# Moving the output stores of a fused attention and FFN kernel to ScalarE, with four loads in flight, DMA transposes in one more step and no decay columns in the last

## The chip, the cores and the metric

The kernel runs on one core of a Trainium2 chip. The metric is the device time of one execution in microseconds (us), as the median of several runs. The profiler's span, from the first to the last record, is shorter than the device time (span 201.4, time 203.12 in the profiled run of the kernel before). Engines: TensorE (PE in the profile; PEld is its weight load), VectorE (DVE), ScalarE (ACT), GpSimd (POOL), SyncE (SP). A q behind the name (SPq, ACTq) is the engine's instruction queue when it issues a DMA.

## The reference

A gated linear attention runs over 768 positions in 4 batches and 8 heads of 48 channels. Its output, 3072 tokens of 384 values, goes through a gated FFN of hidden width 1536.

```python
f = 1.0 / (1.0 + np.exp(-f_logit))
for t in range(S):                                   # S = 768, B = 4, H = 8, D = 48
    state = f[:, :, t, :, None] * state + np.einsum('bhd,bhe->bhde', k[:, :, t], v[:, :, t])
    y[:, :, t] = np.einsum('bhd,bhde->bhe', q[:, :, t], state)
x = y.transpose(0, 2, 1, 3).reshape(B * S, H * D)    # 3072 x 384
out = (np.maximum(x @ w_gate, 0.0) * (x @ w_val)) @ w_out
```

## The kernel before

The kernel takes the 768 positions in six steps of 128 (called step 0 to 5, `c` in the code). In each step and batch it makes prefix sums of the log gates, scaled q and k ("hats"), transposes of these, scores, the output x and a new state; then the FFN of that step for all four batches. Attention of later steps and FFN of earlier ones are interleaved on TensorE.

The kernel first lists its operations with estimated durations, and a list scheduler in the kernel (called the builder here) places them. It works out a plan with a start and an end for every operation, and from that plan fixes one instruction order per engine. On the chip the waits between the lists are semaphores. In the trace of the kernel before, what waited held up what was behind it in its list: ScalarE stood 3.69 us before an exponential whose gate load had not landed (it started at 127.27 us), and the next relu of its list started at 128.39.

Loads of q, k, v and the gate logits f cover two batches each (128 x 16 x 48 floats). A load is paced by the third load before it: the builder does not place it before the planned landing of that one. This "pace" is used in the plan only. There is no semaphore for it.

```python
def load(n, c, b0, b1, after=(), paced=(), eng="SP"):
    ...
    op = add(eng, lambda: e.dma_start(dst, src), [], [f"{n}{c % NL}_{b}" for b in range(b0, b1)],
             occ=..., lat=..., prio=..., after=after, follows=[last] if last else [], paced=paced)
    dma(op, f"{n}{c % NL}_{b0}{b1}", flow, (6.0 if (c, n, b0) == (1, "v", 0) else 2.0) if c else 0.8)

loads.append(load(n, c, b, b + load_batches, loads[-flight:][:1]))      # flight = 3
```

x goes to the FFN transposed. Up to step 3 TensorE transposes it and VectorE copies it out; from step 4 on, a DMA transpose issued by SyncE does it:

```python
if c < first_xbar_x:                                  # first_xbar_x = 4
    ...
    te.transpose(x16()[:, kt * C:(kt + 1) * C], xn[ni][:, kt * C:(kt + 1) * C], ident[:])   # 3 of them
    ...
else:
    op = add("SP", lambda: sy.dma_start(xT[xi][:, :, b * C:(b + 1) * C], xn[ni][:, :], transpose=True), ...)
```

Prefix sum and decay columns, and the store of an output block behind ScalarE's copy of it:

```python
te.matmul(bc.ap[:, 0:HD], tri[:, :], bn[:, :, 0:D])
for p in range(NP):                                   # NP = 4, the decay columns
    mm = te.matmul(bc.ap[:, HD + p:HD + p + 1], bn[:, 2*p:2*p + 2, :]..., ones[:, :])
...
add("ACT", lambda ...: sc.activation(osb[oi][:, n0:n1], o.ap[:, 0:n1 - n0], AF.Copy), ...)
op = add("SP", lambda ...: sy.dma_start(dst, osb[oi][:, n0:n1]), ..., occ=0.2, lat=0.9, prio=P)
```

## Time and profile before

| | before |
|---|---|
| time, median of the first 3 runs | 203.14 us (202.06 to 204.03) |
| span of the profiled run | 201.4 us |
| TensorE busy | 191.7 us, 95% |
| other engines busy | DVE 54%, ACT 57%, POOL 38% |
| bytes read and written in HBM | 25.95 and 4.72 MB |

The page cuts the span into 40 slices and gives the busy share of each in tenths. TensorE is at 9 nearly everywhere after 40 us, so what counts is where it is not. Its waits from 40 us on are few, and the longest is 2.2 us. The profiled run (203.12 us, mean clock 0.992) counts as slow, being 1.5% above the fastest run of this kernel in any set (200.11). Its mean clock of 0.992 is one stretch of 3.41 us at half clock (131.14 to 134.56 us), 1.7 us lost; 17 of the 32 runs of this kernel in the rounds of the experiments had a mean clock of 0.992 or less. In the wait views below the columns are: who waited for whom, the sum in us, how often, and the longest. The profile's own lines of this kernel stand in the prediction.

### The profile page before, as it was taken

How to read it: one execution, taken by the hardware profiler on the slowest of the kernel's cores; microseconds unless marked ns; L12 is line 12 of the kernel's file. 1: busy time of each engine (PE TensorE's matmuls, PEld its weight loads, DVE VectorE, ACT ScalarE, POOL GpSimd, SP SyncE). 2: the span in 40 equal slices, each digit the busy share in tenths (PEclk: the TensorE clock that was granted, in tenths of full speed). 3: DMA queues.
4: the chain of work that ended last, by engine and by line, in shares of the span. 5: the costliest groups of instructions: out<-in, count | busy, mean ns of one | idle time of the engine just before them, and what ended most of it. 6: DMA issues, size and time to landing. Idle time of an engine off the chain costs nothing.

```text
span 201.4 us, 4570 instructions
## 1 busy us (share of the span) xinstructions
PE 191.7 (95%) x1813; PEld 124.4 (62%) x1813; DVE 107.9 (54%) x212; ACT 115.2 (57%) x264; POOL 77.3 (38%) x111
## 2 busy tenths in 40 slices
PE   7989899799999999999999999599999999999995
PEld 5766688676789787855664655245555555444564
DVE  7268575565098988628586846135462334433210
ACT  2976868716678686877677572744354333443412
POOL 5189203563559687772858364053000000000000
PEclk9999999999999999999999999969999999999999
DMA  4999999999999999999989998979222001111113
GB/s 119 234 223 196 198 200 180 204 231 210 230 232 232 158 247 189 221 198 230 192 161 234 159 199 186 189 156 221 77 63 59 24 19 39 39 39 42 39 39 117
DMA packets 116660, 31.35 MB, mean 156 GB/s; under 512 B 109600, under 2 KB 116640, under 8 KB 116640
## 3 DMA queue, kind: packets, MB, share of 16 engines
q1 hardware_dynamic: 112656, 27.53, 67.2%
q0 software_dynamic: 3984, 3.54, 11.0%
q8 instruction: 14, 0.23, 0.5%
q14 instruction: 6, 0.05, 0.1%
HBM read 25.95 MB, written 4.72 MB: 152 GB/s over the span
## 4 chain that ended last, share of the span: by engine, by line
PE 73%; DMA 13%; SPq 8%; ACT 2%; POOL 2%; issue 1%; DVE 0%
PE ps L766 37%; PE ps L789 22%; SPq L399 7%; DMA q_in<-in_q_dram 4%; DMA wv<-in_moe_w_val_dram 4%; PE ps L638 3%; DMA f_in<-in_f_logit_dram 3%; DMA v_in<-in_v_dram 3%; PE ps L615 2%; PE ps L677 2%; PE ps L582 2%; PE ps L673 2%; PE ps L718 1%; PE ps L699 1%; PE ps L584 1%
## 5 line engine op out<-in xcount | busy, mean ns | idle before, releaser
L777 DVE TENSOR_TENSOR gT<-relu,ps 128x256 bf16<-128x256 bf16 (+1 forms) x96 | 52.2, 552 | 59.9 <-PE ps L766 37.2
L766 PE MATMUL ps<-xT,wg 128*128 128x256 bf16 (+1 forms) x288 | 63.1, 328 | 0.3 <-DMA wg<-in_moe_w_gate_dram 0.3
L773 ACT ACTIVATE relu<-ps 128x256 bf16<-128x256 f32 (+1 forms) x96 | 46.3, 490 | 29.1 <-PE ps L766 28.7
L766 PE MATMUL ps<-xT,wv 128*128 128x256 bf16 (+1 forms) x288 | 62.6, 326 | 0.0
L789 PE MATMUL ps<-wo,gT 128*128 128x384 bf16 (+2 forms) x300 | 52.5, 320 | 0.0
L789 PEld LDWEIGHTS ps<-wo,gT 128*128 128x128 bf16 x300 | 27.7, 98 | 17.4
L766 PEld LDWEIGHTS ps<-xT,wg 128*128 128x128 bf16 x288 | 27.0, 98 | 15.6 <-DMA wg<-in_moe_w_gate_dram 0.6
L644 DVE TENSOR_TENSOR ptm<-ps,tri 128x512 bf16<-128x512 f32 x48 | 30.6, 684 | 10.8 <-PE ps L638 10.7
L766 PEld LDWEIGHTS ps<-xT,wv 128*128 128x128 bf16 x288 | 26.1, 98 | 16.0 <-ACT relu L773 0.2
L809 ACT ACTIVATE osb<-ps 128x384 f32<-128x384 f32 (+2 forms) x25 | 11.8, 477 | 30.6 <-PE ps L789 30.5
L602 POOL TENSOR_TENSOR hats<-k_in,expo 128x384 bf16<-128x384 f32 x20 | 20.0, 1000 | 20.3 <-ACT expo L591 20.3
L605 POOL TENSOR_TENSOR hats<-q_in,expo 128x384 bf16<-128x384 f32 x20 | 20.0, 1002 | 2.2 <-DMA q_in<-in_q_dram 2.2
L734 POOL TENSOR_TENSOR st<-ssum,dec 128x384 bf16<-128x384 f32 x16 | 13.3, 830 | 16.2 <-DVE ssum L732 16.2
L455 PE MATMUL ps<-zeros 128*128 128x256 bf16 x89 | 13.0, 301 | 1.1 <-DVE zeros L359 1.1
L691 ACT ACTIVATE xn<-ps 128x384 bf16<-128x384 f32 x20 | 9.8, 488 | 7.1 <-PE ps L677 7.1
L558 POOL CAST vpad<-v_in 128x384 bf16<-128x384 f32 x24 | 12.0, 515 | 3.0 <-DMA v_in<-in_v_dram 2.8
L572 ACT ACTIVATE f_in<-f_in 128x768 f32<-128x768 f32 x10 | 8.4, 838 | 6.4 <-DMA f_in<-in_f_logit_dram 6.4
L591 ACT ACTIVATE expo<-ps 128x384 f32<-128x384 f32 x20 | 9.8, 492 | 3.0 <-PE ps L584 2.9
L455 PEld LDWEIGHTS ps<-zeros 128*128 128x128 bf16 x89 | 9.0, 107 | 3.0 <-DVE zeros L359 1.1
L638 PE MATMUL ps<-qkT 48*128 48x128 bf16 x192 | 8.9, 226 | 1.2 <-ACT qkT L528 0.8
L593 ACT ACTIVATE expo<-ps 128x384 f32<-128x384 f32 x20 | 10.0, 498 | 0.0
L732 DVE TENSOR_TENSOR ssum<-ps,st 128x384 f32<-128x384 f32 x16 | 8.8, 551 | 1.1 <-PE ps L718 0.9
(71 smaller groups left out, 158.3 us busy)
## 6 DMA issues: line engine op xcount, KB each, us to landing
out_dram<-osb SPq DMA_DIRECT2D x23, 192.0 KB, 2.2
f_in<-in_f_logit_dram SPq DMA_DIRECT2D x10, 384.0 KB, 6.2
k_in<-in_k_dram SPq DMA_DIRECT2D x10, 384.0 KB, 6.4
q_in<-in_q_dram SPq DMA_DIRECT2D x10, 384.0 KB, 4.5
v_in<-in_v_dram SPq DMA_DIRECT2D x10, 384.0 KB, 4.8
wg<-in_moe_w_gate_dram POOLq DMA_DIRECT2D x3, 384.0 KB, 7.1
wv<-in_moe_w_val_dram POOLq DMA_DIRECT2D x3, 384.0 KB, 7.4
wo<-in_moe_w_out_dram POOLq DMA_DIRECT2D x3, 384.0 KB, 7.2
```

Of the source, the lines that this page charges most:

```text
L399: op = add(eng, lambda: e.dma_start(dst, src), [], [f"{n}{c % NL}_{b}" for b in range(b0, b1)], occ=(0.8 if eng == "SP" else 0.3) * (b1 - ...
L455: op = add("PE", lambda: te.matmul(cold.ap[:, 0:256], zeros[:, 0:128], zeros[:, :]), ["zeros"], [cold], occ=0.22 if i < 17 else 0.11, lat= ...
L558: add("POOL", lambda: gp.tensor_copy(vout, vin[:, b, :, :].rearrange("p (n j) d -> p n j d", j=2)), [f"v{li}_{b}", f"vpad{vi}"], [f"v_{vi} ...
L602: add("POOL", lambda: gp.tensor_tensor(hk, kin[:, b, :, :], ex[:, 1, :].rearrange("p (h d) -> p h d", h=H), ALU.mult), [f"k{li}_{b}", f"ex ...
L605: add("POOL", lambda: gp.tensor_tensor(hq, qin[:, b, :, :], ex[:, 0, :].rearrange("p (h d) -> p h d", h=H), ALU.mult), [f"q{li}_{b}", f"ex ...
L638: mm = te.matmul(s.ap[:, p * C:(p + 1) * C], qkT[qi][lo:lo + D, 1, p, :], qkT[qi][lo:lo + D, 0, p, :])
L644: add("DVE", lambda j=j, s=s: ve.tensor_tensor(ptm[mi][:, j, :, :], s.ap[:, :].rearrange("p (n t) -> p n t", n=NP), mask, ALU.mult), [s, " ...
L734: add("POOL", lambda: gp.tensor_tensor(t4(s_new), t4(tmp), rate, ALU.mult), [key] + dk, [f"S{b}_{c % 2}"], prio=P + 8, **pool_t(HD))
L766: mm = te.matmul(bank.ap[:, 0:n], wt[:, kt, j * 128:(j + 1) * 128], xT[xi][:, kt, n0:n1], start=(kt == 0), stop=(kt == NK - 1))
L773: add("ACT", lambda: sc.activation(relu[ri][:, 0:n], gate.ap[:, 0:n], AF.Relu), [gate], [f"relu{ri}"], prio=P, **act_t(n))
L777: add("DVE", lambda: ve.tensor_tensor(gT[gi][:, j, n0:n1], relu[ri][:, 0:n], val.ap[:, 0:n], ALU.mult), [val, f"relu{ri}"], [f"gT{gi}_{j}_ ...
L789: mm = te.matmul(o.ap[:, 0:n1 - n0], gT[gi][:, j, b * C:(b + 1) * C], wo[:, j, n0:n1], start=(j == 0), stop=(j == NJ - 1))
```

## The change

Four things were changed together. The stores are issued by ScalarE right behind its own copy, so that SyncE no longer stands waiting for that copy (15 waits in the kernel before, 47.9 us in all, the longest 5.5). Four loads are in flight instead of three. x of step 3 goes by DMA transposes too. The last step, which makes no new state, leaves out its decay columns.

```diff
-    flight = 3
+    flight = 4
-    first_xbar_x = 4
+    first_xbar_x = 3
+    STORE = 'ACT'
...
-                te.matmul(bc.ap[:, 0:HD], tri[:, :], bn[:, :, 0:D])
-                for p in range(NP):
+                mm = te.matmul(bc.ap[:, 0:HD], tri[:, :], bn[:, :, 0:D])
+                for p in range(NP if c < NC - 1 else 0):
...
-            chain("cum", ..., occ=0.29, lat=PE_L,
+            chain("cum", ..., occ=0.29 - (0.12 if c == NC - 1 else 0), lat=PE_L,
...
-            op = add("SP", lambda ...: sy.dma_start(dst, osb[oi][:, n0:n1]), ...,
-                     occ=0.2, lat=0.9, prio=P)
+            op = add(STORE, lambda ...: (sy if STORE == "SP" else sc).dma_start(dst, osb[oi][:, n0:n1]), ...,
+                     follows=first_stores if g == 0 else [], occ=0.2 if STORE == "SP" else 0.4,
+                     lat=0.9 if STORE == "SP" else 1.2, prio=P)
...
+    first_stores = [tails["loadSP"]] if '0' == "1" else []      # empty
```

More of the change, by code (lines that the diff above doesn't have):

```diff
@@ L586, in cum @@
                 return mm
-            chain("cum", "PE", cum, ["tri", "ones", f"bneg{bi}", f"bn{bi}_{bj}"], [bc], occ=0.29, lat=PE_L,
+            chain("cum", "PE", cum, ["tri", "ones", f"bneg{bi}", f"bn{bi}_{bj}"], [bc], occ=0.29 - (0.12 if c == NC - 1 else 0), lat=PE_L,
                 prio=P, opens=[bc])
@@ L811, in ffn_out @@
             dst = bass.AP(tensor=out.tensor, offset=(b * S + g * C) * DM + n0, ap=[[DM, C], [1, n1 - n0]])
-            op = add("SP", lambda dst=dst, oi=oi, n0=n0, n1=n1: sy.dma_start(dst, osb[oi][:, n0:n1]), [f"osb{oi}_{x}" for x in TAIL[:-1] if n0 <= x < n1], [f"out{g}_{b}_{n0}"],
-                     occ=0.2, lat=0.9, prio=P)
+            op = add(STORE, lambda dst=dst, oi=oi, n0=n0, n1=n1: (sy if STORE == "SP" else sc).dma_start(dst, osb[oi][:, n0:n1]), [f"osb{oi}_{x}" for x in TAIL[:-1] if n0 <= x < n1], [f"out{g}_{b}_{n0}"],
+                     follows=first_stores if g == 0 else [], occ=0.2 if STORE == "SP" else 0.4, lat=0.9 if STORE == "SP" else 1.2, prio=P)
             dma(op, f"osb{oi}_{n0}", 0.45 * (n1 - n0) / DM)
+    first_stores = [tails["loadSP"]] if '0' == "1" else []
     OJ = 4
@@ L864, in bass_hgrn2_outer__then__ffn_reglu_kernel @@
             op.val = n
-    stores = [op for op in order["SP"] if op.writes and op.writes[0].startswith("out")]
+    stores = [op for op in order[STORE] if op.writes and isinstance(op.writes[0], str) and op.writes[0].startswith("out")]
     def run(name, eng):
```

## The prediction

> **What bounds the kernel now.** I read the page first (engines, slices, chain), then the stretches in time, then the chain and the SyncE queue around the one place where TensorE stands still.
>
> ```profile
> PE 191.7 (95%) x1813; PEld 124.4 (62%) x1813; DVE 107.9 (54%) x212; ACT 115.2 (57%) x264; POOL 77.3 (38%) x111
> PE   7989899799999999999999999599999999999995
> PEclk9999999999999999999999999969999999999999
> DMA  4999999999999999999989998979222001111113
> ```
>
> TensorE is busy 95% of the span. There is one dip inside, in slice 26 (126 to 131 us), followed by the only slice with a lower granted clock. The DMA row is at 9 until about 137 us. The kernel therefore has three stages: a start to 40 us, which hangs on loads and weights; a middle to about 137 us, in which attention and FFN are interleaved while the loads stream in; and a pure FFN tail, where TensorE is at 10.00 of 10 us in each stretch. The change leaves the start alone: the first output store is at 48.3 us and the first paced load is one of step 2. The stretches of the middle:
>
> ```profile
> 110.00:115.00 5.00, 5.00 (x57) 2.98 (x56) 4.23 (x7) 2.30 (x4) 1.93 (x4) 1.00 0.88 162
> ...
> 120.00:125.00 5.00, 4.73 (x48) 2.79 (x49) 3.30 (x6) 1.09 (x2) 3.10 (x5) 1.00 0.93 204
> 125.00:130.00 5.00, 2.81 (x28) 1.42 (x26) 0.69 (x1) 2.73 (x6) 0.00 (x0) 1.00 1.00 169
> 130.00:135.00 5.00, 5.00 (x40) 2.52 (x39) 1.25 (x2) 3.21 (x8) 2.08 (x3) 0.66 0.94 194
> ```
>
> The columns are window, length, busy time of PE, PEld, DVE, ACT and POOL with counts, clock, DMA share and GB/s. TensorE loses 2.19 us between 125 and 130 and then runs at 0.66. The chain of waits says why:
>
> ```profile
> 118.80 0.61 ACT relu L773
> 119.42 1.22 SPq L812
> 120.64 0.04 issue
> 120.68 1.19 SPq L707
> 121.87 0.04 issue
> 121.92 5.33 DMA f_in<-in_f_logit_dram
> 127.25 0.02 issue
> 127.27 0.84 ACT f_in L572
> ```
>
> The gate load for the second half of step 5 is issued at 121.92. In SyncE's in-order queue it stands behind an output store (which waited for ScalarE, then took 1.22 us) and behind a DMA transpose of 1.19 us. It lands 5.33 us later. ScalarE, also in order, sits 3.69 us on that load with a relu behind it. TensorE comes to the prefix sum of this batch and waits 2.19 us for it, although some 70 us of FFN work stand behind. This is a blocked order, not a lack of work.
>
> [...]the later loads have rows of 48 floats (192 B), and 109600 of the 116660 packets are under 512 B, with at most 247 GB/s in a slice.[...] clock 0.68 from 129.7 to 135[...]
>
> **The change, part by part.**
>
> *No decay columns in step 5.* Four matmuls of one column for each of 4 batches go. The chain shows such a four at 0.09 us (117.93), so 4 x 0.09 = 0.36 us of TensorE. They precede the tail, and TensorE is packed there: all of it counts.
>
> *x of step 3 by DMA transposes.* Four times three TensorE transposes go, 0.19 us a three in the chain (95.96): 0.76 us on a packed engine, so it counts. VectorE loses 4 copies of 0.354 us, which lie beside. Added are 4 DMA transposes on SyncE: the existing eight take 1.18 to 2.09 us of its queue and land after a median of 2.4 us (up to 5.2). That is 5 to 8 us more in SyncE's queue between 88 and 110 us.
>
> *Stores move to ScalarE.* From SyncE go the stores that lie before the late load: 1.15, 0.58, 1.24 and 1.84 us between 78 and 122 us, 4.8 us together. Over that stretch (78.9 to 121.9) the queue's entries sum to 40.9 of 43.0 us, waits included: SyncE is as full as the DMA engines. The four new transposes take back what the four stores give, so SyncE's total hardly falls; what goes is SyncE waiting on copies in ScalarE. ScalarE gains 25 issues. In the quiet tail one takes 0.34 us on SyncE; with the wait for its own copy I estimate 0.5 to 1.2 us of ScalarE each, some 10 us for the dozen in the middle. ScalarE has 7.2 to 7.9 of 10 us busy between 60 and 110, so it becomes some 0.85 full; that should cost TensorE 0 to 1.5 us through late relus and exponentials, say 0.7. In the tail ScalarE is 40% busy and nothing is lost. At the very end the store of the 256 columns is issued by ScalarE between the last two copies: the first ends at 198.78, the matmuls at 199.04, so an issue of 0.34 us from about 198.85 could delay the last copy by 0.1 to 0.2 us[...].
>
> *Four loads in flight.* The pacing is no semaphore; it only sets where the builder places a load in SyncE's order. One more in flight puts the late load about one slot earlier, and the loads of step 5 go out 2 to 6 us apart (107.1, 109.2, 115.1, 118.2, 121.9). It would pass a transpose that waited on GpSimd (the entry of 4.31 us at 110.73) rather than sit behind it. DMA ran at only 162 GB/s in that stretch, so there is room. Three us earlier would cover the idle 2.19 us and with it the throttled stretch: 5.3 us at 0.68 loses 5.3 x 0.32 = 1.7 us. Worth 3.9 us if the gap goes.
>
> Sum: 0.36 + 0.76 = 1.1 us almost certain; 3.9 us for the gap, which I give six chances in ten, or about 2.5 when partial success is counted; minus 0.7 for ScalarE. That is 1.1 + 2.5 - 0.7 = 2.9, and 203.14 - 2.9 = 200.2. I move it to 200.0, because the parts look tuned together. The measured 203.14 against the span of 201.4 is a fixed difference that I carry over.
>
> **Rivals.**
> 1. *The gap stays, because the DMA engines are the bound.* For: their row is at 9 to 137 us, and four transposes are added. Against: 162 to 169 GB/s in the two stretches before and in the gap, against 230 elsewhere. Time: 203.14 - 1.1 + 0.7 = about 202.7; if the gap grows by 2 us, 204 to 205.
> 2. *ScalarE becomes the new blocker.* Its store waits for its own copy, then issues[...], and the relus behind it starve TensorE of its four FFN banks. For: issues of 1.2 us are seen on SyncE. Against: a store is 128 rows of 1536 B on a ring of its own, and TensorE hardly waits for a relu now (under 0.3 us in all). With 12 stores at 0.2 us of TensorE it eats 2.4 us: 201 with the gap closed, 204 with it open.
> 3. *All goes well:* the gap closes and ScalarE costs nothing: 203.14 - 5.0 = 198.1.
> 4. *The new order moves the blockage.* The builder places everything anew, so another load, or an x transpose of step 3, may block. Time as in rival 1.
>
> **Range and chances.** Rival 3 is nearly the floor, as nothing else inside is idle; I put the low end at 197.9. The high end, 203.0, is the gap kept and the small parts won. Faster by over 2% means below 199.08: the gap closed and at most 1 us given back, about one in three. Slower than 207.2 needs a new blockage of over 4 us: 0.06.
>
> **What would show it.** Right: slice 26 at 9 and the clock row without the 6; the gate load of step 5's second half landing 3 us or more before its prefix sum; 64 single-column matmuls in place of 80, 24 TensorE x transposes for 36, 12 x transposes by DMA for 8; stores on ScalarE's queue at 0.35 to 1.2 us each; TensorE busy down by 2 to 3 us (work, and throttled time). Wrong: TensorE idle again for over 1 us anywhere between 45 and 150; waits of TensorE on relu or exponentials summing to more than 1.5 us; or a start that differs from 40.5 us.

## More of the kernel before

The plan's times are estimates of the kernel's author, not measurements.

```python
    # Plan.schedule: when an operation has been placed, its users become ready
    for u in op.users:
        u.n_left -= 1
        if u.deps[op] == "order":
            at = op.start
        elif u.eng == op.eng == "PE":
            at = op.start + op.occ
        else:
            at = op.end                      # for a load: its planned landing
            ...
        u.ready = max(u.ready, at)
```

## The result, and the profile after

The changed kernel took 210.36 us in the median of 6 runs (208.02 to 212.47), the kernel before 203.58 us in the same rounds. The ratio is 1.0305 with a 95% interval of 1.0228 to 1.0382: 3% slower. Here and below, a ratio is the mean time of one kernel's fast runs over that of the other's fast runs of the same rounds, so it is not quite the ratio of the medians quoted.

The page of the changed kernel, its engine line and three of its slice rows:

```profile
PE 194.6 (94%) x1785; PEld 124.6 (60%) x1785; DVE 107.6 (52%) x208; ACT 116.1 (56%) x264; POOL 77.1 (37%) x111
PE   7999899799999995999995979999999999999995
PEclk9999999999999999799999799999999999999999
DMA  4999999999999898999979889999131111111113
```

The one dip of before after 40 us (slice 26) has become three (slices 16, 22 and 24, counted from 1 as in the prediction), and the clock falls twice. TensorE is busy 2.9 us longer with 28 instructions fewer. The stretches show where the time lies. First the kernel before, then the changed kernel; the first number pair is the window and its length, then busy time and instruction counts of PE, PEld, DVE, ACT and POOL, the clock, the DMA share and GB/s:

```profile
40.00:150.00 110.00, 106.90 (x1128) 69.88 (x1129) 68.18 (x128) 68.94 (x168) 59.74 (x75) 0.98 0.98 193
150.00:201.40 51.40, 49.03 (x272) 25.97 (x270) 15.13 (x22) 18.46 (x34) 0.00 (x0) 1.00 0.14 47
```

```profile
40.00:150.00 110.00, 103.37 (x1057) 66.36 (x1058) 65.47 (x121) 67.22 (x163) 59.23 (x75) 0.97 0.99 192
150.00:207.00 57.00, 54.50 (x319) 29.02 (x316) 17.43 (x26) 21.18 (x39) 0.00 (x0) 1.00 0.15 49
```

At 150 us the changed kernel still has 54.50 us of TensorE work ahead, the other 49.03. These 5.5 us are the whole difference of the spans (207.0 - 201.4 = 5.6). So the loss arises in the middle, between 40 and 150 us; start and tail run as before. The DMA engines moved the same 192 to 193 GB/s there, so no bandwidth was gained or lost.

Who held TensorE up? The first fence below is ScalarE's wait on gate loads in the kernel before from 40 us on; the second has the same line and TensorE's three longest waits in the changed kernel:

```profile
ACT f_in L572 <- DMA f_in<-in_f_logit_dram: 6.4, 3, 3.7
```

```profile
ACT f_in L573 <- DMA f_in<-in_f_logit_dram: 12.4, 6, 5.5
...
PE ps L639 <- issue: 3.3, 2, 2.3
...
PE ps L767 <- ACT relu L774: 2.1, 1, 2.1
...
PE ps L616 <- POOL hats L606: 1.2, 1, 1.2
```

ScalarE waits twice as long and twice as often for the gate loads. The chain of waits of the changed kernel shows how such a wait gets to TensorE (start, duration, what):

```profile
72.51 7.25 DMA f_in<-in_f_logit_dram
79.75 0.02 issue
79.78 0.84 ACT f_in L573
80.62 0.02 issue
80.64 0.39 ACT relu L774
81.04 0.05 issue
81.08 0.83 PE ps L767 x6
```

A gate load of step 3 lands at 79.75. ScalarE's list has the exponential of that gate first and a relu of the FFN behind it. TensorE's next matmuls, of L767, wait for this relu, and TensorE has been idle for 2.1 us when they start at 81.08. The relu had nothing to do with the load: it only stood behind it.

The longest gap is another one, before the scores:

```profile
112.03 0.62 PE L639 MATMUL ps<-qkT 48*128 48x128 bf16 x16 [2.26 <-issue]
```

"issue" means that the profile names no releaser. The scores read DMA transposes of scaled q and k; the last one before the gap was issued at 107.76, and those of this stretch land 3.3 to 4.2 us from issue, which fits 112.03. The chain of waits leads from that transpose back over GpSimd and ScalarE to a gate load that landed at 101.87. So this gap, too, goes back to a late gate load, by a longer way; that is inferred from the chain. The gap of 1.06 us at 122.33 stands before scores as well; it was not followed up.

The stores themselves do what was intended. Here is ScalarE's timeline of the changed kernel around one of them:

```profile
107.86 0.49 ACT L810 ACTIVATE osb<-ps 128x384 f32<-128x384 f32 x1
108.38 0.36 ACTq L813 DMA_DIRECT2D out_dram<-osb  x1
108.79 0.60 ACT L774 ACTIVATE relu<-ps 128x512 bf16<-128x512 f32 x1 [0.44 <-PE ps L767]
```

Copy, issue, next relu: from the end of the copy (108.35) to the relu 0.44 us pass, 0.36 of them for the issue.

The decisive reading is a comparison that the page does not make: the builder's plan against the chip. ScalarE starts the exponential of each gate load when that load is there (landed at 127.25 us, started at 127.27, for the last one of the kernel before) or a little later. The planned starts are those that the builder works out when it makes the order; the seen starts are in ScalarE's timeline (us; two loads per step):

| gate load of | 2 | 3 first | 3 second | 4 first | 4 second | 5 first | 5 second |
|---|---|---|---|---|---|---|---|
| before, planned | 63.4 | 72.1 | 82.6 | 92.5 | 101.9 | 112.4 | 123.3 |
| before, seen | 65.0 | 72.3 | 83.1 | 93.0 | 102.6 | 113.3 | 127.3 |
| changed, planned | 61.7 | 69.4 | 76.6 | 85.3 | 96.1 | 106.7 | 117.6 |
| changed, seen | 62.5 | 70.8 | 79.8 | 89.6 | 101.9 | 115.9 | 129.2 |

(The first column is the second load of step 2.) Before, plan and chip agree within 1.6 us up to the last load, which is 4 us late: that is the one gap of before. With the change the plan counts on loads up to 7 us earlier than before. On the chip they come at most 3.3 us earlier in steps 2 to 4 and 2 to 3 us later in step 5. By the end, the plan is 11.6 us ahead of the chip, and every engine's order was made for that plan.

The builder also gives each kernel's planned span. Run again on the kernels' code, it says 198.0 us for the kernel before, 197.4 for the changed one, 198.1 for the kernel before with the fourth load alone and 200.6 for it with the x transposes alone. It thus saw a cost of the x transposes (2.6 us) and none of the fourth load.

### The profile page after: what moved, and what is told of

It reads as the page before. It is cut to its first block, busy times and chain, and to the rows that moved or that the text cites. A ratio compares the mean times of both kernels' runs of the same rounds, so it can differ in the third digit from the quotient of the medians.

```text
span 207.0 us, 4512 instructions
## 1 busy us (share of the span) xinstructions
PE 194.6 (94%) x1785; PEld 124.6 (60%) x1785; DVE 107.6 (52%) x208; ACT 116.1 (56%) x264; POOL 77.1 (37%) x111
## 3 DMA queue, kind: packets, MB, share of 16 engines
q10 hardware_dynamic: 3600, 4.72, 7.2%
HBM read 25.95 MB, written 4.72 MB: 148 GB/s over the span
## 4 chain that ended last, share of the span: by engine, by line
PE 41%; DMA 25%; SPq 24%; ACT 5%; POOL 2%; issue 2%; ACTq 0%
PE ps L767 23%; SPq L400 21%; PE ps L790 15%; DMA f_in<-in_f_logit_dram 11%; DMA q_in<-in_q_dram 4%; DMA wv<-in_moe_w_val_dram 4%; DMA wo<-in_moe_w_out_dram 3%; DMA v_in<-in_v_dram 3%; SPq L625 2%; ACT f_in L573 2%; ACT relu L774 1%; POOL hats L606 1%; PE ps L639 1%; ACT bneg L576 1%; PE ps L583 1%
## 5 line engine op out<-in xcount | busy, mean ns | idle before, releaser
L767 PE MATMUL ps<-xT,wg 128*128 128x256 bf16 (+1 forms) x288 | 63.2, 328 | 2.4 <-ACT relu L774 2.1
L767 PE MATMUL ps<-xT,wv 128*128 128x256 bf16 (+1 forms) x288 | 63.5, 329 | 0.0
L790 PE MATMUL ps<-wo,gT 128*128 128x384 bf16 (+2 forms) x300 | 53.7, 325 | 0.0
L790 PEld LDWEIGHTS ps<-wo,gT 128*128 128x128 bf16 x300 | 28.4, 99 | 18.2 <-issue 1.0
L767 PEld LDWEIGHTS ps<-xT,wg 128*128 128x128 bf16 x288 | 26.9, 98 | 19.4 <-ACT relu L774 2.2
L767 PEld LDWEIGHTS ps<-xT,wv 128*128 128x128 bf16 x288 | 26.8, 98 | 17.3 <-issue 0.3
L456 PE MATMUL ps<-zeros 128*128 128x256 bf16 x89 | 14.1, 318 | 1.1 <-DVE zeros L360 1.1
L592 ACT ACTIVATE expo<-ps 128x384 f32<-128x384 f32 x20 | 9.8, 490 | 5.5 <-PE ps L585 5.3
L456 PEld LDWEIGHTS ps<-zeros 128*128 128x128 bf16 x89 | 9.5, 113 | 3.6 <-DVE zeros L360 1.1
L639 PEld LDWEIGHTS ps<-qkT 48*128 48x128 bf16 x192 | 5.5, 94 | 8.1 <-issue 6.5
```

Source lines behind the costliest of these rows:

```text
L456: op = add("PE", lambda: te.matmul(cold.ap[:, 0:256], zeros[:, 0:128], zeros[:, :]), ["zeros"], [cold], occ=0.22 if i < 17 else 0.11, lat= ...
L639: mm = te.matmul(s.ap[:, p * C:(p + 1) * C], qkT[qi][lo:lo + D, 1, p, :], qkT[qi][lo:lo + D, 0, p, :])
L767: mm = te.matmul(bank.ap[:, 0:n], wt[:, kt, j * 128:(j + 1) * 128], xT[xi][:, kt, n0:n1], start=(kt == 0), stop=(kt == NK - 1))
L790: mm = te.matmul(o.ap[:, 0:n1 - n0], gT[gi][:, j, b * C:(b + 1) * C], wo[:, j, n0:n1], start=(j == 0), stop=(j == NJ - 1))
```

## The experiments

Theory A was that the fourth load in flight moves the plan, not the loads, and that the order built on it blocks TensorE. Theory B was that the four added x transposes do it through SyncE's queue. Theory C was that the stores on ScalarE do it.

### One part at a time

**flight4_alone.** The kernel before with

```diff
-    flight = 3
+    flight = 4
```

> The kernel before with four loads in flight, nothing else of the change. Theory A (with four in flight the builder's own plan expects the gate load of step 5's second half at 114.6 us instead of 123.3, the real loads come no earlier, so every engine's order is built for loads that are not there and TensorE blocks): 207 to 211 us, 2 to 4% slower, TensorE idle 4 us or more between 45 and 150. Theory B (the four added x transposes on SyncE do the damage): 201 to 204, about the same as before. Theory C (stores on ScalarE do it): about the same as before.

Measured: 210.84 us against 203.02, ratio 1.0367 (1.0303 to 1.0432). This one number does more damage than the whole change. ScalarE's wait on the gate loads, and in the next fence the stretch of the middle:

```profile
ACT f_in L572 <- DMA f_in<-in_f_logit_dram: 16.1, 7, 3.6
```

```profile
40.00:150.00 110.00, 100.23 (x1076) 64.92 (x1074) 64.50 (x124) 65.88 (x162) 57.68 (x73) 0.98 0.95 188
```

TensorE does 6.7 us less in the middle than before (100.23 against 106.90), in many small waits. Theory A had said that the loads come no earlier, and in this it was wrong: the late gate load of step 5 did come earlier, as the prediction had it: its exponential started at 122.97 instead of 127.27. But the plan had moved it by more, from 123.3 to 114.6. Earlier loads were no gain, since the order had been drawn up for still earlier ones.

**xdma_alone.** The kernel before with

```diff
-    first_xbar_x = 4
+    first_xbar_x = 3
```

> The kernel before with the x transposes of step 3 by DMA, nothing else. Theory A: 202 to 205 us, within 1.5% of before, since the plan keeps the pacing (load planned at 127.5). Theory B: 207 to 211, since SyncE's queue gets 5 to 8 us longer and the loads stand behind transposes that wait for ScalarE. Theory C: about the same as before.

Measured: 207.17 us against 203.02, ratio 1.0207 (1.0136 to 1.0279). Theory A alone does not cover this: there is a second cost. The chain of waits of this run shows it:

```profile
115.31 0.22 ACT xn L691
115.53 3.66 DMA xT<-xn
119.19 0.05 issue
119.24 1.46 PE ps L766 x3
```

The x of step 3 is ready at 115.53, its DMA transpose lands 3.66 us later, and what TensorE's list has next is matmuls that read it: it stands idle 3.96 us, then takes 1.46 us for three matmuls that otherwise take 0.65, as the clock is at half from 115.3 to 122.1 (a mean of 0.86 from 100 to 125 us). (This profile is of the slowest of the four runs. It also has a gap of 2.34 us at 44 us, on a v load, before any transpose of x of step 3; that one can hardly be the change's.) With TensorE's own transposes the same step took 0.19 us and a VectorE copy of 0.35 us.

**stores_act_and_decay.** The changed kernel with

```diff
-    flight = 4
+    flight = 3
-    first_xbar_x = 3
+    first_xbar_x = 4
```

> The changed kernel with three loads in flight and x of step 3 by TensorE: only the stores on ScalarE and the missing decay columns remain. Theories A and B: 201 to 203.5 us, 0 to 1% faster than before (0.36 us of matmuls saved, SyncE freed of stores). Theory C: 206 or more, with TensorE waiting for relus behind store issues.

Measured: 202.45 us against 203.02, ratio 0.9966 (0.9913 to 1.0020): the same. Theory C falls.

**after_flight3.** The changed kernel with

```diff
-    flight = 4
+    flight = 3
```

> The changed kernel with three loads in flight again. Theory A: most of the loss comes back, 202 to 205 us. Theory B: it stays at 207 to 211. Theory C: it stays at 207 to 211.

Measured: 206.40 us against 203.02, ratio 1.0160 (1.0079 to 1.0242). About half of the loss comes back; that is less than theory A had expected (202 to 205). What stays fits the x cost: TensorE waits 2.4 us for x in this profile.

**after_xpe.** The changed kernel with

```diff
-    first_xbar_x = 3
+    first_xbar_x = 4
```

> The changed kernel with x of step 3 by TensorE again: four in flight, stores on ScalarE, no decay columns. Theory A with the x transposes as a second cost that overlaps the first: 207.5 to 210.5 (flight4_alone less 0.4 to 1). If the two costs simply add: 206 or less.

Measured: 208.30 us against 202.53, ratio 1.0271 (1.0182 to 1.0361). Next to four in flight, the x transposes cost no more than the noise (1.0305 with them, in another set of rounds). The two costs overlap: the changed kernel's profile has no wait of TensorE for x over 0.2 us.

### Is it the order, or are four loads in flight bad in themselves?

The next two kernels change only what the builder believes. A load's users are counted ready some time after (or before) its planned landing; the pacing of the loads themselves keeps the planned landing.

```diff
-                    at = op.end
+                    at = op.end + (op.slack if u.deps[op] != "pace" else 0.0)
...
         tails["load" + eng] = op
+        op.slack = (0, 0, 1, 2, 3, 4)[c]       # flight4_honest, beside flight = 4
+        op.slack = (0, 0, -2, -3, -3, -3)[c]   # flight3_hopeful, beside flight = 3
```

**flight4_honest**

> flight4_alone (210.8 us) with the same four loads in flight and the same transfers, but the builder is told that a load of step 2, 3, 4, 5 is usable 1, 2, 3, 4 us after its planned landing; its plan then starts the gate exponentials within 2 us of where the chip started them in flight4_alone (planned 81.1, 91.0, 102.0, 112.8, 124.7; seen 80.0, 90.1, 101.8, 113.2, 123.0). Theory A (the order, built on loads planned too early, is what blocks TensorE): 201 to 204.5 us. Rival D (four loads in flight[...] hold up transposes and stores, whatever the order): 208 or more.

Measured: 203.78 us against 202.53, ratio 0.9992 (0.9857 to 1.0126). The ratio rests on two fast runs, 200.77 and 203.74; the other two, 203.82 and 204.52, count as slow. Most of the 3.7% is gone; up to 1.3% may be left. The middle of the profiled run, the fastest of the four:

```profile
40.00:150.00 110.00, 106.94 (x1128) 69.39 (x1126) 68.53 (x129) 69.57 (x168) 57.06 (x73) 1.00 0.96 193
```

TensorE does as much there as before the change (106.94 against 106.90), and ScalarE has no wait on a gate load in the list any more. The exponentials started when they had started in flight4_alone or up to 1.3 us off (seen 80.0, 89.7, 100.7, 112.1, 124.3).

**flight3_hopeful**

> The kernel before, three in flight, with the plan told the opposite: loads of steps 2 to 5 usable 2 to 3 us before their planned landing (gate exponentials planned at 75.7, 83.2, 93.8, 103.9, 113.8). Theory A: it slows like flight4_alone, 206 to 211 us. Rival D: about the same as before, 202 to 204.5.

Measured: 209.70 us against 202.53, ratio 1.0358 (1.0267 to 1.0449). ScalarE's wait on the gate loads, and the middle:

```profile
ACT f_in L574 <- DMA f_in<-in_f_logit_dram: 9.6, 7, 3.5
```

```profile
40.00:150.00 110.00, 101.83 (x1088) 66.07 (x1089) 65.75 (x125) 66.36 (x162) 60.10 (x76) 0.97 1.02 190
```

With three loads in flight, the same transfers and the same work, a plan that hopes for earlier loads costs as much as the fourth load in flight did. Together the two runs show that the order, built on planned landings that the chip does not keep, is what costs the time. Rival D (that four loads hold up transposes and stores, whatever the order) falls as the main cause. There is one order on each side; how far a new order alone scatters the time was not measured.

**after_honest.** The whole change, with `op.slack = (0, 0, 1, 2, 3, 5)[c]`.

> The whole change (210.4 us), every transfer kept, but the builder is told that a load of step 2, 3, 4, 5 is usable 1, 2, 3, 5 us after its planned landing (its own span becomes 199.5 us against 198.0 for the kernel before). Theory A with the x transposes as a separate cost: 203.5 to 207 us: the loss from the blocked order goes, that of the x transposes stays. If the order were the only cost: 201 to 203. If it did nothing here: 208 or more.

Measured: 208.11 us against 203.71, ratio 1.0196 (1.0097 to 1.0295). In absolute terms this is outside the 203.5 to 207 of theory A and just inside the "208 or more" that stood for "did nothing", with a kernel before that was also slower in these rounds. As a ratio it is near xdma_alone (1.0207), but its interval overlaps that of the whole change (1.0228 to 1.0382), so the time alone does not show that the part of the order went. The profile speaks for it: ScalarE has no wait on a gate load, and TensorE waits 3.2 us for x. (It, too, has a gap on a v load, 1.73 us at 44 us, that can hardly be the change's.)

### Why do the x transposes cost anything?

**x_both_ways.** The kernel before, in which step 3 makes x by TensorE and also issues the four DMA transposes, into a spare buffer. The output is right; the extra copy is thrown away.

```diff
+                if c == 3:
+                    op = add("SP", lambda: sy.dma_start(xdum[b % 2][:, :, :], xn[ni][:, :], transpose=True),
+                             [f"xn{ni}"], [f"xdum_{b % 2}"], prio=P + 8, occ=1.2, lat=1.2)
+                    dma(op, f"xdum_{b % 2}", 0.4, late)
```

> The kernel before, in which x of step 3 is still made by TensorE, with the four DMA transposes of step 3 issued as well, into a buffer that nobody reads. It keeps their time in SyncE's queue and on the DMA engines and takes away the wait for their result. Theory X1 (xdma_alone loses its 4 us because FFN work of step 3 waits for x to land, 3.96 us in one place): 202 to 204.5 us, within 0.8% of before. Theory X2 (the transposes hold up the loads behind them in SyncE's queue): 206 to 208, as xdma_alone.

Measured: 204.40 us against 203.71, ratio 1.0066 (0.9981 to 1.0152). SyncE's queue shows that the transposes took the time there that I had worried about:

```profile
101.08 3.49 SPq L708 DMA_TRANSPOSE xdum<-xn  x2
...
110.02 4.46 SPq L708 DMA_TRANSPOSE xdum<-xn  x2
```

These 8 us of SyncE's queue (waits included) cost 0.7%, with 1 inside the interval. xdma_alone lost 2.1% although it also saved TensorE 0.76 us, 0.4%. What is left, 2.1 + 0.4 - 0.7 = 1.8%, fits theory X1: FFN work waits for x to land. This is a subtraction across two sets of rounds, and the two intervals just overlap; what is shown directly is the wait of 3.96 us in the profile.

### The two small parts, and a better version

**stores_alone** has the stores on ScalarE and keeps the decay columns.

> The kernel before with only the stores on ScalarE (decay columns kept). If the decay columns are worth their 0.36 us and no more: 202.3 to 203.3 us, 0 to 0.3% faster than before. If ScalarE paid for the stores: 204 or more.

Measured: 204.50 us against 203.71, ratio 1.0078 (1.0009 to 1.0148). That is slower than I expected, in the range named for a ScalarE that pays for the stores, and did not fit stores_act_and_decay. Three kernels were therefore run in five rounds on one chip.

**stores_again**, the same kernel:

> stores_alone once more, in five rounds. If ScalarE pays nothing for the stores: within 0.5% of before. If the 0.8% was real: 0.5 to 1% slower again.

**decay_same_order**, the same without the 16 matmuls, planned as if they were there:

```diff
-                for p in range(NP):
+                for p in range(NP if c < NC - 1 else 0):
```

> stores_again without the 16 single-column matmuls of step 5, the plan still counting their time, so that every engine's order is the same but for them. If the matmuls are worth their busy time: 0.36 us, 0.1 to 0.3% faster than stores_again. If they stand in the blocked stretch (the prefix sums of step 5), up to 1 us.

**both_small_again**, which is stores_act_and_decay:

> stores_act_and_decay once more: the same matmuls gone, and the builder knows it, so TensorE's order differs in step 5. If order noise made the difference: 0.5% or more faster than decay_same_order. If the sets of runs differed: as decay_same_order within 0.3%.

| | ratio to before | 95% interval |
|---|---|---|
| stores_again | 1.0029 | 0.9957 to 1.0101 |
| decay_same_order | 1.0007 | 0.9959 to 1.0056 |
| both_small_again | 0.9979 | 0.9930 to 1.0027 |

By these ratios the matmuls are worth 0.2% (0.0022 x 201 us = 0.4 us), the shorter plan another 0.3%; all three intervals include 1. Both parts are too small to be told from nothing here. But the first row rests on two of six runs: the other four, 204.03 to 205.24 us at mean clocks of 0.983 to 0.992, count as slow (median of all 204.05; before had 200.81). None of the six of decay_same_order does. So whether the 0.8% of stores_alone is real, and whether leaving out the decay columns gains more than 0.4 us by sparing a fall of the clock, stays open.

**best_guess** is stores_act_and_decay with a corrected plan for the last step only, `op.slack = (0, 0, 0, 0, 0, 2)[c]`, since only there plan and chip were apart.

> stores_act_and_decay (202.45 us) with the plan told that the loads of step 5 are usable 2 us later than planned (its gate exponentials of step 5 were planned at 112.9 and 123.9 and seen at 115.4 and 127.4). Theory A: the 1.25 us idle and the low clock after it go, 199 to 201.5 us. Rival D: unchanged, 202 to 203.

Measured: 199.87 us against 202.53, ratio 0.9863 (0.9793 to 0.9934). Two slice rows of its page:

```profile
PE   7979799999999999999999997998999999999994
PEclk9999999999999999999999999999999999999999
```

The clock does not fall in any of the four runs. That is no gain of the corrected plan: it did not fall in those of stores_act_and_decay either.

**best_again**, the same kernel in the five rounds:

> best_guess once more. If its gain holds: 1 to 2% faster than before and at least 0.7% faster than both_small_again.

Measured: 199.92 us against 200.81, ratio 0.9951 (0.9898 to 1.0003). This kernel took 199.9 us both times; the kernel before took 202.5 us in one set of rounds and 200.8 in the other. In the first set six of its seven runs had a mean clock of 0.992 or less, in the second two of eleven; best_guess and best_again had 1.000 in all ten. So the size of the gain goes with how often the clock fell before. It is the fastest version here, 0.5 to 1.4% faster than before, but the second interval just touches no gain at all, and both hopes set on the second run (1 to 2% over before, at least 0.7% over both_small_again) failed; over the latter it is 0.3%.

**best_guess4** is best_guess with four loads in flight and `op.slack = (0, 0, 1, 2, 3, 4)[c]`.

> Stores on ScalarE, no decay columns, x of step 3 by TensorE, four loads in flight, with loads of step 2, 3, 4, 5 planned usable 1, 2, 3, 4 us later. Theory A: 199 to 202 us, no worse than best_guess (199.9 us) by more than 1%; four in flight then gives nothing over three, because the DMA engines were full already. If four in flight had a gain of its own: under 199.

Measured: 204.44 us against 203.71, ratio 1.0088 (1.0029 to 1.0148). My expectation missed by over 2 us. In this profile TensorE waits 4.3 us in all for DMA transposes of scaled q and k before scores. flight4_honest has gaps of 1.2 and 1.6 us before scores too, there behind ScalarE. So rival D may hold in a small way: with four loads planned ahead, something between 0 and 2% stays even when the landings are planned right. I did not find out whether it is the loads in front of these transposes in SyncE's queue or again the order.

## Why the prediction was wrong, point by point

**What bounds the kernel before** was read rightly: one blocked place, from a gate load that was late, and a DMA row at 9 to 137 us. One reading is off: "162 to 169 GB/s in the two stretches before and in the gap, against 230 elsewhere". The two stretches before the gap had 190 and 204 GB/s, and the five stretches of 10 us from 60 to 110 had 197 to 214, so there was less room for an earlier load than it says. Unblocking it by a corrected plan was worth 0.3% on one chip (0.9979 to 0.9951) and 1.0% between two sets of runs (0.9966 to 0.9863), 0.6 to 2 us in place of the 3.9 that I put on it, and hardly clear of the noise.

**Decay columns**: predicted 0.36 us; 64 single-column matmuls instead of 80 as foretold; measured 0.4 us in the same order, within the noise and against two fast runs. Not contradicted.

**Stores on ScalarE**: predicted to cost TensorE 0.7 us. Measured 0.3% and 0.8% in two sets, with 1 inside the first interval and just outside the second. Each issue took 0.34 us, and with the handover 0.44 us where it was looked at, in place of the 0.5 to 1.2 estimated. The stores went over a DMA queue of their own, q10 on the page (4.72 MB), where the kernel before has none. Rival 2 did not come true as meant: TensorE did wait 2.1 us for a relu, but that relu stood behind a gate load and not behind a store.

**x of step 3 by DMA**: this step failed in its sign. The prediction counted 0.76 us of TensorE's time as won and looked for the cost in SyncE's queue. It never followed x to its reader. That path got longer by a landing of 3.66 us in place of 0.19 us of transposes and a copy of 0.35 us, at a place where TensorE's list held nothing else. Measured: +2.1% alone, 4 us.

**Four loads in flight**: this is the step that failed most, by its wait and not by a size. The prediction said of the pacing that "it only sets where the builder places a load in SyncE's order". That is only half of what it does. The planned landing also makes every user of the load ready in the plan, and so fixes the order of ScalarE, TensorE, VectorE and GpSimd. The gain of 3.9 us was reasoned from the load alone: it would land 3 us earlier. In flight4_alone it did, by 4.3 us, and the kernel became 3.7% slower, because its users had been moved up by 8.7 us. In the full change the same load even came 1.9 us later (exponential at 129.17 against 127.27). flight4_honest and flight3_hopeful show the cause from both sides.

**The rivals**: rival 4, "the new order moves the blockage", is what happened. Its size was wrong. I priced it as one blockage of the old kind, at most 205 us. It became three: the loads followed the plan only in part, and the error grew from 0.8 to 11.6 us. A warning was in the prediction's own words: the DMA row is at 9 to 137 us, and the bytes per second stayed the same with four loads in flight (193 and 192 GB/s). That this is why the loads lag behind the plan was not tested.

**The sum**: 2.9 us won were forecast, 6 to 7 us were lost. Of the signs named for "wrong", the first came true: TensorE idle for over 1 us between 45 and 150, three times (2.12, 2.26 and 1.06 us). So did the second: waits on relus and exponentials sum to over 1.5 us (2.1 + 0.3 + 0.2).

## What to carry to other kernels

In a kernel whose instruction order comes from a plan, compare planned and seen starts of a few landmark operations before touching a parameter. A parameter that changes the plan's belief about transfers changes the order of all engines, and the transfers need not follow: here they moved by 4.3 us where the plan moved by 8.7. Correcting that belief by 2 us in one step, with the two small parts, gave the fastest version here, though its gain is near the noise. When work is moved from an engine to a DMA, follow the result to its reader and count the landing, not the issue.

## What else the traces show

- The clock fell to 0.50 for 3.41 us after gaps of 2.19 us (kernel before) and of 2.12 and 2.26 us (changed kernel). It stayed at 1.00 from 40 to 150 us in stores_again, with a gap of 2.7 us. So the length of the gap alone did not decide. (The 0.68 that the prediction read is a mean over a longer stretch.) The two falls of the changed kernel lie 30.72 us apart, nine times 3.41. Of the stretches of that length, counted from a fall, the one that ended at a fall had TensorE busy for 40% in the kernel before and for 38% and 34% in the changed kernel. From 40 to 150 us, each of the other 56 stretches at full clock in these two traces was at 75% or more. In these two traces, then, the falls go with the stretches of lowest busy share; why the gap of stores_again brought none was not shown.
- With the DMA row at 9, a DMA transpose of x (128x384) landed 3.66 us after its source was ready (xdma_alone; 2.3 to 5.2 us from issue in the kernel before), which cost 3.96 us of TensorE.
- With the order fixed ahead of time, the same work with the same three loads in flight took 1.0358 times as long (flight3_hopeful), only because the plan believed in earlier loads.
